# Weight blocks behind the rows' gather, one tile of softmax sums, a fourth staging tile

## The chip, the cores and the metric

The kernel runs on one core of one Trainium2 chip. The metric is the device time of one execution in microseconds (us): the median of several runs for the time, and one profiled execution for everything that is read from the trace. The engines are TensorE (PE; PEld its weight loads), VectorE (DVE), ScalarE (ACT), GpSimd (POOL) and SyncE (SP, which here issues most DMAs). Each takes its instructions in order.

## The reference

Three stages follow each other over 4 x 576 = 2304 tokens of width 512.

```python
# attention, 4 batches x 8 heads, 576 positions, head width 64, factor 4
q_d, k_d, v_d = (mean over groups of 4 positions of q, k, v)
out_d   = softmax(q_d k_d^T / 8) v_d                    # pooled part: 144 x 144
out_up  = repeat(out_d, 4, axis=positions)
scores  = where(abs(i - j) < 4, q k^T / 8, -1e9)        # banded part
x       = out_up + softmax(scores) v                    # heads side by side: 2304 x 512
# a dense product layer
x       = (((x @ w1) * (x @ w2)) @ w3) @ w_out          # inner width 1024
# a mixture of 8 experts, each token goes to one
e       = argmax(x @ w_gate)
g       = max(softmax(x @ w_gate)) * sigmoid((x @ w_output_gate)[e])
out     = g * relu(x @ e_w1[e]) @ e_w2[e]               # 512 -> 1024 -> 512
```

## The kernel before, in words

Every large product is made of three matmuls (`mm3`, lines 399 to 401): both factors are split into a high part (a cast on ScalarE) and a low part (a subtraction on VectorE or GpSimd), and high x high, high x low and low x high are added in PSUM.

**Weights at the front.** The four weights of the dense layer come in as 64-bit floats. `f64_bits` (lines 128 to 130) makes 32-bit floats of them with three VectorE instructions a tile. w_out is converted first, with w_gate and w_output_gate folded in (`gate_step`), then w3 is multiplied with it (`w3_part`, `wc_half`, `wc_out`) into `wc`, then w1 and w2 go through `w_part` in 16 pieces: `f64_bits` into a tile `wf`, a cast on ScalarE (line 377) and a subtraction on GpSimd (line 378). The tile `wf` of `w_part` and the tile `a` of `g1_step` (line 427: ScalarE's copy of the first product; line 428: VectorE multiplies with the second; 430: cast; 432: subtraction, on GpSimd for most) take turns in the staging tiles with the tag `t2k`, 2 KB a partition each, of which there are three. The tiles `wot`, `gs`, `ci` and `cj` have the same tag.

**Attention.** Two heads are one unit, 16 units in all. A unit goes through five steps, `a_T`, `a_S1`, `a_S2`, `a_V1`, `a_V2`, spread by hand between the steps of the dense layer (`step`). `a_S1` makes both score blocks: the banded one in `sm`, the pooled one in `ed`; ScalarE takes exponentials, and for `ed` it also writes the row sums to `zd` (line 217). `a_S2` reduces `sm` to its sums `su` (VectorE, 226), adds the epsilon and inverts (227, 228), and multiplies `sm` by the result on GpSimd (229); `zd` goes through the same two VectorE instructions (230, 231; there the factor 4 of the pooled mean is put in) and `ed` is multiplied on GpSimd (232). `a_V1` transposes `ed` on TensorE and `sm` on VectorE (244), `a_V2` multiplies with v; ScalarE copies the pooled output to `up` (272) and VectorE adds the two parts into `xr` (280).

**Dense layer.** Six groups of 384 tokens: `g1_step` (48 in all) and `g2_step`, which stores the rows of y to DRAM (`yd`; the second half of the width also to `yh`), and collects the gate logits. `route_*` make the tables of which token goes to which expert.

**The start of the experts.** The last part of the program is ordered by hand: `ordered(...)` puts a step's TensorE instructions behind those of the one before, `after(last)` puts ScalarE's and VectorE's behind a pair of theirs, `behind(rows, load)` makes a load wait until a gather has landed. Everything else is laid out by a planner that runs at build time with simulated times. The rows of the first expert are gathered from DRAM by GpSimd (`x_gather`, line 677) in two halves of the width, the second half first, and transposed into `xT` by `x_prep` (TensorE 695; ScalarE's cast and VectorE's subtraction 699). Expert weights come in blocks (r, m, i): expert rank r, first (m = 0) or second (m = 1) layer, block i of 4, 512 KB each; `ew_load` issues the load on SP (708 for m = 0, 711 for m = 1), `ew_split` casts on ScalarE (720) and subtracts on VectorE or GpSimd (722). The second-layer blocks of the first expert, (0,1,0) to (0,1,2), are loaded into the three parts of a tile `early`, the others into four tiles `raw`. While the first halves of the rows are on their way, `ga_part` runs the products of six column blocks with the second halves. `route_gate`, `gate_rhs` (573) and `route_gtab` (582, 585) make the table of gate values, and `route_gates` adds its parts (638, tile `b_gt`). Then the first halves are transposed (3 blocks of up to 128 rows, 2 PSUM tiles with the tag `tr`), `ga_step` finishes the first layer, `gb_step` does the second, and the loop over the other experts goes on; `x_gather(r + 1)` is issued on GpSimd behind the instruction called `first`.

Of the kernel before, what the change touches and what calls it, by code (L numbers as in the profile page):

```python
# [20 lines left out]
P = 128  # L21
# [3 lines left out]
G = 384  # L25
# [23 lines left out]
def attention_moe_kernel(ctx: ExitStack, tc: tile.TileContext, q, k, vw_in, v4_in, w1, w2, w3, w_out,  # L49
# [29 lines left out]
    ci = mt([P, P], I32, "ci", tag="t2k", bufs=3)  # L79
    cj = mt([P, P], F32, "cj", tag="t2k", bufs=3)  # L80
# [65 lines left out]
    for t in (kz, *qTs, bd, qz):  # L146
        nc.gpsimd.memset(t, 0.0)
    st = {}
# [40 lines left out]
    def a_S1(u):  # L189
# [24 lines left out]
        zd = at([96, 3], F32, "zd", bufs=2)  # L214
# [4 lines left out]
        d.update(sm=sm, ed=ed, zd=zd)  # L219

    def a_S2(u):
        d = st[u]
        sm, ed = d["sm"], d["ed"]
        su = at([P, 6, 2], F32, "su", bufs=2)
        sd = d["zd"]
        nc.vector.tensor_reduce(out=su, in_=sm, axis=AX.X, op=ALU.add)
        nc.vector.tensor_scalar(su, su, 1e-9, None, op0=ALU.add)
        nc.vector.reciprocal(su, su)
        nc.gpsimd.tensor_tensor(sm, sm, su.unsqueeze(3).to_broadcast([P, 6, 2, 32]), op=ALU.mult)
        nc.vector.tensor_scalar(sd, sd, 4.0, 4e-9, op0=ALU.mult, op1=ALU.add)  # L230
        nc.vector.reciprocal(sd, sd)
        nc.gpsimd.tensor_tensor(ed, ed, sd.unsqueeze(2).to_broadcast([96, 3, 144]), op=ALU.mult)
# [24 lines left out]
    def a_V2(u):  # L257
# [14 lines left out]
        nc.scalar.copy(out=up, in_=xl[0][:, 288:432])  # L272
# [43 lines left out]
    def gate_step(f, gps, src):  # L316
# [11 lines left out]
        wot = mt([P, KD, P], F32, "wot", tag="t2k", bufs=3)  # L328
# [5 lines left out]
    def gate_finish(gps):  # L334
        gs = mt([P, 2 * P], F32, "gs", tag="t2k", bufs=3)
# [32 lines left out]
    def w_part(m, f):  # L368
# [4 lines left out]
        t = mt([P, 512], F32, "wf", tag="t2k", bufs=3)  # L373
# [41 lines left out]
    def g1_step(g, f):  # L415
        xh, xl = xg[g]
        pp = []
        for m in range(2):
# [6 lines left out]
            if m == 0:  # L425
                a = mt([P, G], F32, "a", tag="t2k", bufs=3)
                nc.scalar.copy(out=a, in_=ps[:, 0:G])  # L427
# [253 lines left out]
    def x_prep(r, b, k0=0, k1=KD):  # L681
# [10 lines left out]
        ps = at_psum()  # L692
        pv = ps[:, 0:512].rearrange("p (k n) -> p k n", k=KD)
        for kk in range(k0, k1):
            nc.tensor.transpose(pv[:, kk, 0:n], t[0:n, P * kk:P * kk + P], ident[0:n, 0:n])  # L695
        c = slice(P * b, P * b + n)
        x = pv[:, k0:k1, 0:n]
# [291 lines left out]
    behind(rows, ew_load(0, 1, 0, early[:, 0]))  # L989
# [5 lines left out]
    store = ordered(g2_step, NG - 1, 2, 0)  # L995
    with tc.issue_after(store.ins):
        ew_load(0, 1, 1, early[:, 1])
    rows = x_gather(0, 0)
    behind(rows, ew_load(0, 0, 3))
    last = ordered(x_prep, 0, NBLK[0] - 1, KD // 2, KD)  # L1000
    with after(last):
# [5 lines left out]
        ew_split(0, 1, 0)  # L1007
# [4 lines left out]
    with tc.issue_after(rows.ins):  # L1012
        first = ew_split(0, 1, 1)
    for b in range(NBLK[0]):
        last = ordered(x_prep, 0, b, 0, KD // 2)
    with after(last):
        ew_split(0, 0, 3)
    for i in range(2, 4):
        behind(rows, ew_load(0, 1, i, early[:, 2] if i == 2 else None))
# [90 lines left out]
```

## Time and profile before

| | |
|---|---|
| median of 3 runs | 733.3 us (730.72 to 735.91) |
| profiled execution | 732.85 us |
| its span, first to last instruction | 731.0 us |
| busy: TensorE | 696.0 us, 95% |
| busy: VectorE | 434.1 us, 59% |
| busy: GpSimd | 324.7 us, 44% |
| busy: ScalarE | 282.5 us, 39% |
| mean granted TensorE clock | 0.99 |
| moved by DMA | 97.72 MB |

Times in the trace count from the first instruction. The profiled execution's own time is its span and 1.85 us around it. A busy TensorE is the time in which a matmul was under way, so what it lacks to the span are its waits. In a timeline, the bracket at the end of a line is how long the engine had been idle before the instruction, and what released it.

### The profile page before, as it was taken

The page shows a single profiled execution, that of the slowest core. Times are in us where ns is not written, and L with a number is a line of the kernel's source. Part 1 is how long each engine was busy: PE and PEld are TensorE (multiplying, and loading weights), DVE is VectorE, ACT ScalarE, POOL GpSimd, SP SyncE. Part 2 cuts the span into 40 slices and gives each one's busy share as a digit, 9 for nine tenths or more (in the row PEclk, how much of TensorE's full clock was granted, in tenths as well). Part 3 has the DMA queues.
Part 4 walks back from the last instruction along what each step waited for, and adds up shares of the span by engine and source line. Part 5 has one row for each costly group of instructions (what it writes and reads, how often), then busy time and mean ns, then how long its engine had stood idle before and what let it go on. Part 6 is the DMA issues. An engine that isn't in the chain of part 4 may idle for free.

```text
span 731.0 us, 14702 instructions
## 1 busy us (share of the span) xinstructions
PE 696.0 (95%) x5710; PEld 666.4 (91%) x5711; DVE 434.1 (59%) x924; ACT 282.5 (39%) x640; POOL 324.7 (44%) x306
## 2 busy tenths in 40 slices
PE   4889899999999999999999999979999999999995
PEld 3679788889999999999999999969999999999994
DVE  8999898862664547254352343475766656766830
ACT  3466356431354135135123121345353444544510
POOL 6866686930362155042011120166484655764611
PEclk9999999999999999999999999989999999999998
DMA  8987957512153032111100101665444744645301
GB/s 323 274 247 234 293 175 230 168 57 66 50 142 119 30 109 83 65 39 45 52 15 1 44 1 52 199 232 195 154 165 147 255 163 167 206 165 204 117 25 41
DMA packets 38264, 97.72 MB, mean 134 GB/s; under 512 B 6018, under 2 KB 12930, under 8 KB 38192
## 3 DMA queue, kind: packets, MB, share of 16 engines
q1 hardware_dynamic: 34768, 86.82, 36.5%
q0 software_dynamic: 3424, 9.93, 3.8%
q8 instruction: 46, 0.75, 0.4%
q14 instruction: 26, 0.21, 0.1%
HBM read 84.93 MB, written 12.29 MB: 133 GB/s over the span
## 4 chain that ended last, share of the span: by engine, by line
PE 73%; DMA 8%; POOL 5%; DVE 5%; issue 5%; ACT 2%; SPq 0%; POOLq 0%; DVEq 0%; ACTq 0%
PE g L399 22%; PE g L401 21%; PE g L400 21%; DMA v<-in_v_dram 3%; DMA kz<-in_k_dram 2%; PE at L197 1%; PE tr L695 1%; PE at L269 1%; PE at L209 1%; PE tr L788 1%; POOL v L236 1%; DMA f<-in_moe_w_dram 1%; POOL W L378 1%; PE at L265 1%; POOL out_dram L778 1%
## 5 line engine op out<-in xcount | busy, mean ns | idle before, releaser
L399 PE MATMUL g<-xh,W 128*128 128x384 f32 x384 | 131.7, 343 | 1.5 <-ACT a L427 1.4
L401 PE MATMUL g<-xh,W 128*128 128x384 f32 x384 | 129.4, 337 | 0.7 <-POOL W L378 0.7
L400 PE MATMUL g<-xl,W 128*128 128x384 f32 x384 | 129.3, 337 | 0.0
L722 DVE TENSOR_TENSOR W<-raw,W 128x1024 fp32r<-128x1024 f32 x32 | 87.9, 2779 | 34.0 <-ACT W L720 25.1
L722 POOL TENSOR_TENSOR W<-raw,W 128x1024 fp32r<-128x1024 f32 x29 | 82.9, 2877 | 36.2 <-ACT W L720 36.2
L432 POOL TENSOR_TENSOR h<-a,h 128x384 fp32r<-128x384 f32 x30 | 30.8, 1026 | 123.9 <-ACT h L430 123.7
L399 PE MATMUL g<-xT,W 128*128 128x288 f32 (+6 forms) x256 | 81.7, 319 | 1.0 <-ACT xT L699 1.0
L400 PE MATMUL g<-xT,W 128*128 128x288 f32 (+6 forms) x256 | 79.8, 312 | 0.0
L401 PE MATMUL g<-xT,W 128*128 128x288 f32 (+6 forms) x256 | 79.5, 311 | 0.0
L399 PEld LDWEIGHTS g<-xh,W 128*128 128x128 f32 x384 | 72.2, 188 | 4.2 <-ACT a L427 2.1
L401 PEld LDWEIGHTS g<-xh,W 128*128 128x128 f32 x384 | 72.1, 188 | 1.5 <-POOL W L378 1.3
L400 PEld LDWEIGHTS g<-xl,W 128*128 128x128 f32 x384 | 72.2, 188 | 0.0
L399 PE MATMUL g<-h,W 128*128 128x288 f32 (+5 forms) x224 | 69.9, 312 | 0.0
L400 PE MATMUL g<-wc,h 128*128 128x272 f32 (+1 forms) x240 | 68.4, 285 | 0.0
L399 PE MATMUL g<-wc,h 128*128 128x272 f32 (+1 forms) x240 | 68.3, 285 | 0.0
L400 PE MATMUL g<-h,W 128*128 128x288 f32 (+5 forms) x224 | 68.0, 303 | 0.0
L401 PE MATMUL g<-h,W 128*128 128x288 f32 (+5 forms) x224 | 68.0, 303 | 0.0
L401 PE MATMUL g<-wc,h 128*128 128x272 f32 (+1 forms) x240 | 67.7, 285 | 0.0
L428 DVE TENSOR_TENSOR a<-g,a 128x384 f32<-128x384 f32 x48 | 26.7, 555 | 62.8 <-PE g L401 58.6
L720 ACT CAST W<-raw 128x1024 fp32r<-128x1024 f32 x61 | 59.8, 1046 | 9.8 <-DMA raw<-in_moe_w_dram 5.6
L748 ACT ACTIVATE h<-g 128x288 fp32r<-128x288 f32 (+6 forms) x64 | 27.9, 436 | 77.2 <-PE g L401 71.7
L778 POOL DMA_INDIRECT out_dram<-orow,b_si x24 | 23.4, 976 | 62.9 <-DVE orow L777 59.4
(255 smaller groups left out, 1696.7 us busy)
## 6 DMA issues: line engine op xcount, KB each, us to landing
raw<-in_moe_w_dram SPq DMA_DIRECT2D x61, 512.0 KB, 4.2
f64w<-in_moe_w_dram SPq DMA_DIRECT2D x16, 512.0 KB, 4.5
f<-in_moe_w_dram SPq DMA_DIRECT2D x16, 512.0 KB, 3.5
vw<-in_vw_dram SPq DMA_DIRECT2D x16, 384.0 KB, 4.0
kc<-in_k_dram SPq DMA_DIRECT2D x16, 288.0 KB, 3.2
qT<-in_q_dram SPq DMA_DIRECT2D x16, 288.0 KB, 4.1
kz<-in_k_dram SPq DMA_DIRECT2D x32, 144.0 KB, 4.0
v<-in_v_dram SPq DMA_DIRECT2D x16, 288.0 KB
```

Of the source, the lines that this page charges most:

```text
L197: end = nc.tensor.matmul(sl[32 * j:32 * j + 32, b], qT[:, 24 * g:24 * g + 32], kz[:, :, 24 * g:24 * g + 32], start=True, stop=True, tile_p ...
L209: nc.tensor.matmul(sd[:, qb], qf[:, 96 * qb:96 * qb + 96], d["kd"], start=True, stop=True)
L236: nc.gpsimd.tensor_tensor(vt, vt, v4[:, :, 2:4], op=ALU.add)
L399: nc.tensor.matmul(ps, whi, xhi, start=first, stop=False)
L400: nc.tensor.matmul(ps, whi, xlo, start=False, stop=False)
L401: return nc.tensor.matmul(ps, wlo, xhi, start=False, stop=last)
L428: nc.vector.tensor_tensor(a, pp[1][:, 0:G], a, op=ALU.mult)
L432: eng.tensor_tensor(lo, a, hi.bitcast(F32), op=ALU.subtract)
L720: nc.scalar.copy(out=hi, in_=t)
L722: ins = eng.tensor_tensor(lo, t, hi.bitcast(F32), op=ALU.subtract)
L748: return nc.scalar.activation(out=t[:, 0, 0:C], in_=ps[:, 0:C], func=AF.Relu), nc.vector.scalar_tensor_tensor(t[:, 1, 0:C], ps[:, 0:C], 0. ...
L778: ins = nc.gpsimd.indirect_dma_start(out=out, out_offset=bass.IndirectOffsetOnAxis(ap=rt["si"][0:n, r, b:b + 1], axis=0), in_=t[0:n], in_o ...
```

## The change

Four edits, made together:

- The staging tag `t2k` has four tiles in place of three.
- The sums of both softmaxes of a unit lie in one tile of 15 columns, one tile for even and one for odd units: 12 for the banded part, 3 for the pooled one. One VectorE instruction adds the epsilon to all of them and one inverts all. The tiles are filled with ones at the start. `ed` is scaled by ScalarE, in three instructions with a scale per row, where GpSimd multiplied it. The factor of a quarter goes into ScalarE's copy `up`.
- The loads of (0,1,0) and (0,1,1), issued before the gather of the first halves, now come behind it, and their splits behind the transposes of the first halves.
- For the transposes of the first halves, two PSUM tiles are taken at once, and blocks 0 and 1 write different columns of the first.

The diff, without the hunks that only put `bufs=4` in place of `bufs=3` elsewhere:

```diff
@@ -145,6 +145,9 @@
     qz = at([P, 2, 144], F32, "qz")
     for t in (kz, *qTs, bd, qz):
         nc.gpsimd.memset(t, 0.0)
+    sums = [at([P, 15], F32, f"sum{i}") for i in range(2)]
+    for t in sums:
+        nc.vector.memset(t, 1.0)
     st = {}
 
     def burst():
@@ -211,25 +214,24 @@
         md = at([96, 3], F32, "md")
         nc.vector.tensor_reduce(out=md, in_=sd, axis=AX.X, op=ALU.max)
         nc.scalar.mul(md, md, -1.0 / 128)
-        zd = at([96, 3], F32, "zd", bufs=2)
+        zd = sums[u % 2][0:96, 12:15]
         nc.scalar.activation(out=sm, in_=sm, func=AF.Exp, scale=0.125)
         for qb in range(3):
             nc.scalar.activation(out=ed[:, qb], in_=sd[:, qb], func=AF.Exp, scale=1.0 / 128,
                                  bias=md[:, qb:qb + 1], accum_out=zd[:, qb:qb + 1])
-        d.update(sm=sm, ed=ed, zd=zd)
+        d.update(sm=sm, ed=ed)
 
     def a_S2(u):
         d = st[u]
         sm, ed = d["sm"], d["ed"]
-        su = at([P, 6, 2], F32, "su", bufs=2)
-        sd = d["zd"]
+        sums_u = sums[u % 2]
+        su = sums_u[:, 0:12].rearrange("p (b h) -> p b h", b=6)
         nc.vector.tensor_reduce(out=su, in_=sm, axis=AX.X, op=ALU.add)
-        nc.vector.tensor_scalar(su, su, 1e-9, None, op0=ALU.add)
-        nc.vector.reciprocal(su, su)
+        nc.vector.tensor_scalar(sums_u, sums_u, 1e-9, None, op0=ALU.add)
+        nc.vector.reciprocal(sums_u, sums_u)
         nc.gpsimd.tensor_tensor(sm, sm, su.unsqueeze(3).to_broadcast([P, 6, 2, 32]), op=ALU.mult)
-        nc.vector.tensor_scalar(sd, sd, 4.0, 4e-9, op0=ALU.mult, op1=ALU.add)
-        nc.vector.reciprocal(sd, sd)
-        nc.gpsimd.tensor_tensor(ed, ed, sd.unsqueeze(2).to_broadcast([96, 3, 144]), op=ALU.mult)
+        for qb in range(3):
+            nc.scalar.activation(out=ed[:, qb], in_=ed[:, qb], func=AF.Copy, scale=sums_u[0:96, 12 + qb:13 + qb])
         v4 = d["v4"]
         vd = at([72, 2, 2, D], F32, "vd", bufs=2)
         vt = v4[:, :, 0:2]
@@ -269,7 +271,7 @@
                     nc.tensor.matmul(xl[c // 3][64 * h:64 * h + 64, 96 * (c % 3):96 * (c % 3) + 96], vw[:, c, D * h:D * h + D],
                                      bd[:, 2 * c + h, :], start=True, stop=True)
         up = at([P, 144], F32, "up")
-        nc.scalar.copy(out=up, in_=xl[0][:, 288:432])
+        nc.scalar.mul(up, xl[0][:, 288:432], 0.25)
         for a in range(2):
             n = b * S + 288 * a
             assert G * split[0] >= n + 288 - RING
...
@@ -370,7 +372,7 @@
         if f % 2 == 0:
             for z in range(2):
                 wab[m][z][f // 2] = w_tile(8 * m + 4 * z + f // 2, [P, 1024])
-        t = mt([P, 512], F32, "wf", tag="t2k", bufs=3)
+        t = mt([P, 512], F32, "wf", tag="t2k", bufs=4)
         f64_bits(src, t.bitcast(U32))
         hi, lo = (wab[m][z][f // 2].rearrange("p (k c) -> p k c", k=KD)[:, :, P * (f % 2):P * (f % 2) + P] for z in range(2))
         x = t.rearrange("p (k c) -> p k c", k=KD)
@@ -678,7 +680,7 @@
                                                in_offset=bass.IndirectOffsetOnAxis(ap=idx, axis=0))
         return ins
 
-    def x_prep(r, b, k0=0, k1=KD):
+    def x_prep(r, b, k0=0, k1=KD, bank=None):
         C = CAPS[r]
         if r not in xT:
             if r == 0:
@@ -689,12 +691,12 @@
                 xT.update({i: (odd[:, 0], odd[:, 1]) for i in range(1, E, 2)})
         n = min(P, C - P * b)
         t = rt["xr"][r, b]
-        ps = at_psum()
-        pv = ps[:, 0:512].rearrange("p (k n) -> p k n", k=KD)
+        pv = (at_psum() if bank is None else bank)[:, 0:512].rearrange("p (k n) -> p k n", k=KD)
+        o = 0 if bank is None else (b % 2) * (k1 - k0)
         for kk in range(k0, k1):
-            nc.tensor.transpose(pv[:, kk, 0:n], t[0:n, P * kk:P * kk + P], ident[0:n, 0:n])
+            nc.tensor.transpose(pv[:, o + kk, 0:n], t[0:n, P * kk:P * kk + P], ident[0:n, 0:n])
         c = slice(P * b, P * b + n)
-        x = pv[:, k0:k1, 0:n]
+        x = pv[:, o + k0:o + k1, 0:n]
         hi, lo = xT[r][0][:, k0:k1, c], xT[r][1][:, k0:k1, c]
         return nc.scalar.copy(out=hi, in_=x), nc.vector.tensor_tensor(lo, x, hi.bitcast(F32), op=ALU.subtract)
 
@@ -986,17 +988,16 @@
     ordered(g2_step, NG - 1, 0, 0)
     rows = x_gather(0, 1)
     behind(rows, ew_load(0, 0, 2))
-    behind(rows, ew_load(0, 1, 0, early[:, 0]))
     ew_split(0, 0, 0)
     ordered(g2_step, NG - 1, 1, 0)
     for b in range(NBLK[0] - 1):
         ordered(x_prep, 0, b, KD // 2, KD)
     ew_split(0, 0, 1)
-    store = ordered(g2_step, NG - 1, 2, 0)
-    with tc.issue_after(store.ins):
-        ew_load(0, 1, 1, early[:, 1])
+    ordered(g2_step, NG - 1, 2, 0)
     rows = x_gather(0, 0)
     behind(rows, ew_load(0, 0, 3))
+    for i in range(2):
+        behind(rows, ew_load(0, 1, i, early[:, i]))
     last = ordered(x_prep, 0, NBLK[0] - 1, KD // 2, KD)
     with after(last):
         ew_split(0, 0, 2)
@@ -1004,19 +1005,20 @@
         rhs = mt([P, CPG, 2 * E * NC], F32R, "rhs", tag="W15")
         for c in range(CPG):
             gate_rhs(NG - 1, c, rhs[:, c])
-        ew_split(0, 1, 0)
     for f in range(6):
         ordered(ga_part, 0, f, KD // 2, KD, True, False)
     ordered(route_gtab, NG - 1, rhs)
     route_gates()
-    with tc.issue_after(rows.ins):
-        first = ew_split(0, 1, 1)
+    banks = [at_psum() for _ in range(2)]
     for b in range(NBLK[0]):
-        last = ordered(x_prep, 0, b, 0, KD // 2)
+        last = ordered(x_prep, 0, b, 0, KD // 2, banks[b // 2])
     with after(last):
         ew_split(0, 0, 3)
     for i in range(2, 4):
         behind(rows, ew_load(0, 1, i, early[:, 2] if i == 2 else None))
+    for i in range(2):
+        with after(last), tc.issue_after(rows.ins):
+            first = ew_split(0, 1, i)
     for r in range(E):
         for f in range(KF):
             last = ordered(ga_step, r, f)
```

## Rows read from the trace of the kernel before

**Rows 1.** Two windows: length, busy us (instructions) per engine, granted clock, DMA share, GB/s

```profile
20.00:160.00 140.00, 127.89 (x1371) 116.24 (x1372) 123.40 (x256) 73.10 (x199) 99.99 (x111) 0.99 0.70 216
160.00:470.00 310.00, 310.00 (x2598) 302.61 (x2597) 138.72 (x442) 93.28 (x249) 75.69 (x88) 1.00 0.20 60
```

**Rows 2.** Waits before 160 us: engine, line, releaser, us in total, times, longest

```profile
DVE wf L130 <- POOL h L432: 2.5, 2, 1.9
...
PE g L399 <- ACT a L427: 1.4, 2, 0.8
...
PE g L401 <- POOL W L378: 0.7, 2, 0.4
```

**Rows 3.** Timeline of VectorE, 99 to 100 us: start, length, instruction, idle before and releaser

```profile
99.11 0.15 DVE L230 TENSOR_SCALAR zd<-zd 96x3 f32<-96x3 f32 x1
99.19 0.15 DVE L227 TENSOR_SCALAR su<-su 128x12 f32<-128x12 f32 x1
```

**Rows 4.** Groups before 160 us: line, instruction, count, busy us, mean ns, idle before

```profile
L217 ACT ACTIVATE ed<-at,md 96x144 f32<-96x144 f32 x24 | 8.8, 370 | 0.1
...
L232 POOL TENSOR_TENSOR ed<-ed,zd 96x432 f32<-96x432 f32 x8 | 7.2, 905 | 3.7 <-ACT wc L363 2.0 <-DVE zd L231 1.6
```

**Rows 5.** Timeline of SP's DMA issues around the gathers, 450 to 515 us

```profile
468.39 1.01 SPq L711 DMA_DIRECT2D early<-in_moe_w_dram  x1
469.50 1.57 SPq L457 DMA_DIRECT2D yd<-yb  x2
```

**Rows 6.** Timeline of GpSimd, 476 to 482 us

```profile
476.13 1.23 POOL L677 DMA_INDIRECT xr<-yd,b_g  x1 [11.47 <-DMA early<-in_moe_w_dram]
477.66 0.95 POOL L677 DMA_INDIRECT xr<-yd,b_g  x1 [0.30 <-issue]
...
479.92 2.35 POOL L722 TENSOR_TENSOR W<-early,W 128x1024 fp32r<-128x1024 f32 x1
```

**Rows 7.** Timeline of VectorE, 475 to 483 us

```profile
475.29 1.23 DVE L722 TENSOR_TENSOR W<-early,W 128x1024 fp32r<-128x1024 f32 x1 [0.43 <-ACT W L720]
...
477.91 1.20 DVE L573 TENSOR_TENSOR rhs<-r_o,r_eb 128x288 fp32r<-128x288 f32 x3
...
480.10 2.34 DVE L638 TENSOR_TENSOR b_gt<-tab 128x144 f32<-128x144 f32 x1
```

**Rows 8.** Timeline of TensorE, 478 to 484 us

```profile
478.51 1.06 PE L582 MATMUL tr<-rhs,rb 128*128 128x288 f32 x3 [1.23 <-DVE rhs L573]
...
480.56 0.45 PE L695 MATMUL tr<-ident,xr 128*128 128x128 f32 x2 [0.77 <-DMA xr<-yd,b_g]
482.83 0.58 PE L695 MATMUL tr<-ident,xr 96*128 96x96 f32 x2 [1.82 <-DVE xT L699]
483.82 0.66 PE L399 MATMUL g<-xT,W 128*128 128x352 f32 x1 [0.41 <-ACT xT L699]
```

**Rows 9.** Timeline of ScalarE: the cast of the last late block of w1

```profile
485.34 1.04 ACT L720 CAST W<-raw 128x1024 fp32r<-128x1024 f32 x1 [1.57 <-DMA raw<-in_moe_w_dram]
```

**Rows 10.** Windows around the expert start, and one early stretch (columns of rows 1)

```profile
75.00:80.00 5.00, 2.17 (x53) 1.98 (x57) 4.75 (x10) 2.60 (x10) 2.55 (x5) 1.00 1.02 246
...
477.00:484.00 7.00, 2.77 (x12) 1.43 (x10) 6.28 (x16) 1.22 (x4) 5.90 (x6) 0.77 0.32 95
484.00:487.60 3.60, 3.60 (x12) 3.49 (x13) 1.34 (x3) 1.82 (x3) 2.51 (x3) 0.50 1.01 390
487.60:495.00 7.40, 7.40 (x48) 7.40 (x48) 4.67 (x9) 4.16 (x8) 2.41 (x1) 1.00 1.01 353
```

**Rows 11.** Timeline of all engines, 41 to 43 us: one PSUM bank written and read

```profile
41.67 0.67 PE L269 MATMUL at<-bd,vw 128*64 128x96 f32 x12
...
42.38 0.28 ACT L272 COPY up<-at 128x144 f32<-128x144 f32 x1 [1.25 <-PE at L269]
```

**Rows 12.** DMA issues, 450 to 467 and 480 to 500 us: count, size, landing

```profile
yh<-yb SPq DMA_DIRECT2D x2, 128.0 KB, 2.6
...
xr<-yd,b_gi POOLq DMA_INDIRECT x4, 7.8
```

More of the change, by code (lines that the diff above doesn't have):

```diff
@@ L78, in attention_moe_kernel @@
     i8 = i128[:, 0:E]
-    ci = mt([P, P], I32, "ci", tag="t2k", bufs=3)
-    cj = mt([P, P], F32, "cj", tag="t2k", bufs=3)
+    ci = mt([P, P], I32, "ci", tag="t2k", bufs=4)
+    cj = mt([P, P], F32, "cj", tag="t2k", bufs=4)
     nc.vector.memset(ones, 1.0)
@@ L327, in gate_step @@
             nc.tensor.transpose(ps[:, P * n:P * n + P], t[:, P * n:P * n + P], ident)
-        wot = mt([P, KD, P], F32, "wot", tag="t2k", bufs=3)
+        wot = mt([P, KD, P], F32, "wot", tag="t2k", bufs=4)
         nc.scalar.copy(out=wot, in_=ps.rearrange("p (n f) -> p n f", n=KD))
@@ L334, in gate_finish @@
     def gate_finish(gps):
-        gs = mt([P, 2 * P], F32, "gs", tag="t2k", bufs=3)
+        gs = mt([P, 2 * P], F32, "gs", tag="t2k", bufs=4)
         nc.scalar.copy(out=gs, in_=gps[:, 0:2 * P])
@@ L425, in g1_step @@
             if m == 0:
-                a = mt([P, G], F32, "a", tag="t2k", bufs=3)
+                a = mt([P, G], F32, "a", tag="t2k", bufs=4)
                 nc.scalar.copy(out=a, in_=ps[:, 0:G])
```

## The prediction

> **What bounds the kernel now.** I read the busy times by window first. From 160 to 470 us TensorE is busy in all of 310.00 us [rows 1]: nothing that another engine does there can shorten the run. From 20 to 160 us TensorE is busy 127.9 of 140, so 12.1 us are to be had, and VectorE, busy 123.4, is nearest to full; GpSimd has 100.0 and ScalarE 73.1 [rows 1]. Then the waits of that stretch: TensorE waited 1.4 us for ScalarE's copy `a` and 0.7 us for a GpSimd weight split, and VectorE 2.5 us, in two waits, for GpSimd's line 432, which frees a 2 KB staging tile [rows 2]. Last the timelines around the start of expert 0, since the other hole lies there: from 477 to 484 TensorE is busy 2.77 us of 7.0, and in the 3.6 us behind it the granted clock is 0.50, the 1.2 GHz level [rows 10].
>
> That second hole reads as a chain. SP issues the early block of w2 at 468.39, and the last two stores of y only from 469.50 on, ending at 471.07 [rows 5]. The gather of the rows' first halves, which needs those stores, starts at 476.13, after 11.47 us of idle GpSimd put down to the early blocks [rows 6]. Meanwhile VectorE splits the early block at 475.29, ahead of the gate chain, whose `rhs` ends at 479.11 [rows 7]; TensorE waits 1.23 us for it, then 0.77 for rows of block 1, then 1.82 for VectorE, and resumes expert 0 at 483.82 [rows 8]. VectorE was late because `b_gt` at 480.10 took 2.34 us [rows 7], under GpSimd's split of the second early block, 479.92 for 2.35 [rows 6]; the larger `rhs` products took 1.20/3 = 0.4 us each [rows 7].
>
> **The fourth staging tile (A).** It removes no instruction. VectorE's 2.5 us of waits were for a staging tile, and TensorE's 1.4 + 0.7 = 2.1 us came at the end of the weight conversion, which VectorE paces [rows 2]. Bounds: 0, if the planner, which orders all engines by simulated times at build, spends the tile otherwise, or if the next weights, loaded only as older ones are converted, are late instead; and -2.1. I take **-1.5**, nearer to the whole, since the wait removed from VectorE is longer than TensorE's.
>
> **The softmax (B).** Eight of the sixteen units fall before 160 us [rows 4]; the other eight lie under the full TensorE and are worth nothing. Each loses two small VectorE instructions (`zd` at lines 230 and 231). One occupies 0.08 us from start to start and 0.15 by its length [rows 3]: 8 x 2 x 0.08 = 1.3 us, at most 8 x 2 x 0.15 = 2.4. GpSimd loses 8 x 0.905 = 7.2 us; ScalarE gains 24 scalings, for which the nearest row is the exponential of the same shape, 0.370 us [rows 4], so up to 8.9 us on an engine with 67 to spare. In a unit's own chain three times 0.37 = 1.1 stand in place of 0.905, 0.2 worse, or 8 x 0.2 = 1.6 us if every unit were on the path. VectorE's add of epsilon now also waits for the three exponentials; behind it queue its weight conversions. Before, `zd` was ready 0.08 us ahead of that add [rows 3], so I cost the wait at nothing; without that cover it is up to three exponentials, 1.1 us, a unit. From +1.6 to -2.4 I take **-1.0**, VectorE's time, because VectorE is the fullest engine. The factor 0.25 rides on a copy that is there anyway. **C**: two fills of 15 columns on VectorE at the start, 0.1 at most, since even the 3-column `zd` lasts 0.15 [rows 3]: **+0.1** for both.
>
> **The rows earlier (D).** The early loads of (0,1,0) and (0,1,1) go behind the gather. So the last store, issued by 471.07, meets an emptier queue; a store of this size landed in 2.6 us [rows 12], at 473.7. The gather then starts 2.4 us earlier than 476.13. In it, block 1 started 1.53 us after block 0, and its rows were used at 480.56, 2.9 us after its start; all three were issued by 479.9 [rows 6, 8]. New: block 0 lands at 476.6, block 1 at 478.1, block 2 at about 479.4. The gate chain loses the 1.23 us split in front of it, the length of TensorE's wait, so its 1.06 us product runs from 477.3 to 478.35. Block 0's transposes follow. Blocks 0 and 1 now share a PSUM bank. The row of before in which a bank's other columns are still being written has ScalarE start at 42.38, behind matmuls that end at 42.34, though they write other columns than it reads [rows 11]; so block 1 waits for both readers of block 0, about 1.5 us from its start (TensorE resumed 0.99 us after block 2's transposes began, with one reader between [rows 8]; the second reader half as much again): 479.85, then 0.45, then block 2 at 480.3, and 0.99 later, 481.3, TensorE resumes. Gain 483.8 - 481.3 = **-2.5**. If the store lands no earlier, the shorter chain alone leaves block 2 at 476.13 + 5.7 = 481.8 and TensorE at 482.8: -1.0. If block 1 need not wait, block 2's landing at 479.4 sets it, TensorE resumes at 480.4: -3.4.
>
> The Trainium skill (PSUM — Partial Sum Buffer, "PSUM bank collisions raise a hardware error") speaks against this part: it has accesses of two engines guarded by bank and quadrant, not by address. By it the saving of a buffer is no saving of a wait, D = -2.5; by addresses alone it would be -3.4. The trace agrees with the guard, as the 42.38 row shows.
>
> **The clock (E).** Twelve matmuls took 3.60 us at 0.50 against 7.40/48 = 0.154 each at 1.00: 12 x (0.300 - 0.154) = 1.75 us lost [rows 10]. TensorE had been busy 2.77 of 7 us before that; earlier, 2.17 of 5 us left the clock at 1.00 [rows 10]. After the change it would be busy 1.06 + 0.45 + 0.45 + 0.4 of the 4.0 us to 481.3, which lies between: half, **-0.9**, with 0 and -1.75 as ends.
>
> **The weights later (F).** On SP the loads now wait for the gather's landing, 479.4, all four of w2 behind (0,0,3); expert 1's loads queue behind them. 0.524 MB at 390 GB/s [rows 10] is 1.34 us a block; with the store's 2.6 taken as the latency in front, (0,0,3) lands at 483.3, (0,1,1) at 486.0, (0,1,3) at 488.7. TensorE needs 60 matmuls x 0.155 before the second layer, 490.6, and 18 more, 493.4, before the last block. That block: cast 1.04 [rows 9], GpSimd split 2.35, done at 492.1 in 1.3 us of cover. In GpSimd's queue the gather of expert 1 stands behind the split of (0,1,1), done at 489.4; 1.5 us each [rows 6], one gather ahead of the last split costs 0.2, two 1.7. Rows for expert 1 are needed at 490.6 + 24 x 0.155 = 494.3: with the 2.9 us landing nothing, with 7.8, the median of 480 to 500 us [rows 12], 497.2 and 2.9 us of wait. ScalarE's relus may stand behind a cast; four PSUM buffers cover that. I take **+0.7**, nearer to none, because by 489 most of the loads have passed.
>
> Sum: -1.5 - 1.0 + 0.1 - 2.5 - 0.9 + 0.7 = -5.1. The profiled execution took 732.85 (span 731.0, 1.85 around it), 0.45 below the median 733.3: 732.85 - 5.1 = **727.75**.
>
> **Rivals.** (1) *The front gives nothing*: the planner lays out the order anew, the longer ScalarE chain eats VectorE's relief, A and B cancel. For it: eight units at +0.2; against: VectorE's buffer waits are plain in the rows. Without -2.5: 730.2. (2) *Slower: expert 1's rows come late.* GpSimd takes the split of (0,1,3) first, the gather starts at 492.1 and lands after 7.8 us, 499.9: TensorE waits 5.6 us behind the first part of expert 0's second layer, and the clock falls again, so E is 0. -1.5 - 1.0 + 0.1 - 2.5 + 5.6 + 1.75 = +2.45: 735.3. It decides from a landing at about 499.4, where wait and clock outweigh the -4.9. For it: 1 MB of loads moved into a stretch with the DMA at 390 GB/s; against: the queue is nearly drained by then. (3) *More than forecast*: both waits of TensorE at the front go (-2.1), B in full (-2.4), no half clock (-1.75), D as forecast, F 0: -8.65, 724.2. (4) *It does not do what it says*: the store lands no earlier behind the load (0,0,2), D = -1.0, E = 0: 730.15.
>
> **How the numbers follow.** Forecast 0.52, between 725 and 730; rivals (1) and (4) together 0.23, near 730; (3) 0.16; (2) 0.09. One per cent, about what a measurement of this kernel tells from no change, is 7.3 us: 726.0 and 740.6. Faster by over 1%: all of (3) and a third of the forecast that lies low, 0.16 + 0.15 = 0.31; slower by over 1%: only (2) with more on top, 0.04; the rest 0.65. The range reaches from beyond (3), where D's -3.4 adds to it, 723.3, to between (1) and (2), 733.5; what lies outside are most of (2) and the ends of (3).
>
> **What would show it.** Right: no VectorE wait at line 130 for line 432; L232 gone from GpSimd and three short ScalarE instructions a unit in its place; first-half gather starting within 3 us of the last store; `b_gt` near 0.3 us; TensorE resuming some 4 us after its first-half products, with less or no half clock. Wrong: a wait of TensorE at line 695 for rows of expert 1, or at line 399 or 401 for a split, between 490 and 500 us; or as much idle before 160 us as now.

## The result and the profile after

| | before | after |
|---|---|---|
| median of 20 runs | 733.75 us (730.21 to 737.59) | 737.16 us (733.87 to 743.62) |
| ratio of the times, 95% interval | | 1.0069 [1.0048, 1.0089] |
| profiled execution | 732.85 us | 739.67 us, span 737.8 |
| busy: TensorE, VectorE | 696.0, 434.1 us | 699.0, 425.1 us |
| busy: GpSimd, ScalarE | 324.7, 282.5 us | 308.7, 296.4 us |

By the ratio, the change made the kernel slower by 0.69%, some 5 us (the two medians differ by 3.4 us), where 5.6 us less than the median was forecast. The measured time lies above the range.

The windows of after that answer to [rows 1], and three from the start of the experts on:

```profile
20.00:160.00 140.00, 125.33 (x1344) 114.50 (x1345) 119.09 (x236) 78.30 (x217) 91.40 (x103) 0.96 0.69 215
160.00:470.00 310.00, 310.00 (x2588) 302.31 (x2587) 136.63 (x426) 100.30 (x273) 68.73 (x81) 1.00 0.19 59
...
485.00:495.00 10.00, 9.27 (x57) 8.98 (x57) 6.01 (x7) 7.26 (x12) 3.62 (x2) 1.00 1.00 390
500.00:505.00 5.00, 2.40 (x9) 2.33 (x10) 0.00 (x0) 0.45 (x1) 4.99 (x4) 0.64 0.44 116
505.00:510.00 5.00, 5.00 (x23) 5.00 (x23) 1.92 (x2) 1.63 (x2) 3.14 (x2) 0.68 0.94 343
```

The front shows the main loss. VectorE has 4.3 us less to do than in [rows 1] (119.09 for 123.40) and GpSimd 8.6 us less (91.40 for 99.99), as the diff promises. Yet TensorE gets 27 fewer matmuls done (1344 for 1371), in 2.6 us less busy time at a mean clock of 0.96 instead of 0.99. The relieved engines stand idle, and TensorE waits more. The clock has a share beside the waits. From 20 to 60 and from 60 to 100 us, before:

```profile
20.00:60.00 40.00, 34.71 (x458) 30.24 (x460) 37.68 (x89) 23.28 (x70) 31.52 (x40) 0.96 0.84 256
60.00:100.00 40.00, 36.91 (x470) 34.46 (x467) 35.62 (x77) 21.05 (x64) 24.56 (x30) 1.00 0.84 259
```

After:

```profile
20.00:60.00 40.00, 35.08 (x455) 31.16 (x456) 33.38 (x79) 23.16 (x71) 28.16 (x36) 0.91 0.84 246
60.00:100.00 40.00, 35.60 (x439) 33.04 (x438) 32.29 (x66) 24.10 (x67) 20.15 (x25) 0.96 0.75 240
```

That is some 7 us more at the 1.2 GHz level (the mean clock is lower by 0.05 and 0.04 over 40 us each, and that level is half of the other), so by estimate up to 3.5 us lost, of one size with the 2.6 us of waits. Since TensorE is full from 160 us to the experts, whatever is left undone at 160 comes back behind it, one for one. The cleanest clock for this is the first gather of the new rows on GpSimd, which starts when the last products of the dense layer are nearly through. Before:

```profile
461.01 1.16 POOL L677 DMA_INDIRECT xr<-yh,b_gi  x1 [23.88 <-PE g L400]
```

After (lines are shifted by 2 to 3 in this kernel):

```profile
465.30 1.17 POOL L679 DMA_INDIRECT xr<-yh,b_gi  x1 [23.88 <-PE g L402]
...
478.58 0.96 POOL L679 DMA_INDIRECT xr<-yd,b_g  x1 [9.62 <-DVE r_gs L561]
...
491.23 2.39 POOL L724 TENSOR_TENSOR W<-early,W 128x1024 fp32r<-128x1024 f32 x1 [9.06 <-ACT W L722]
493.77 1.78 POOL L679 DMA_INDIRECT xr<-yd,b_gi  x1
...
498.30 1.87 POOL L679 DMA_INDIRECT xr<-yd,b_gi  x1 [0.30 <-issue]
500.18 7.00 POOL L724 TENSOR_TENSOR W<-raw,W 128x1024 fp32r<-128x1024 f32 x3
```

That gather is 4.29 us late, so by then 4.3 of the 6.8 us between the two profiled spans are lost. The waits of the front that are new or longer (engine, line, releaser, us in total, times, longest):

```profile
ACT ed L234 <- DVE sum L231: 9.2, 4, 6.1
...
DVE sT L246 <- POOL sm L232: 4.2, 4, 1.5
...
PE at L267 <- ACT pt L256: 2.3, 1, 2.3
...
PE at L200 <- DVE wc L366: 2.1, 1, 2.1
```

VectorE's wait for line 432 fell from 2.5 us [rows 2] to 0.3, nearly as forecast. In its place ScalarE stands 9.2 us in front of the new scalings, and TensorE now waits for attention copies and for `wc`. The longest of ScalarE's waits can be followed on VectorE:

```profile
105.49 0.55 DVE L229 TENSOR_REDUCE sum<-sm 128x12 f32<-128x384 f32 x1
...
106.88 5.04 DVE L395 TENSOR_TENSOR xl<-xr,xh 128x384 fp32r<-128x384 f32 x2
111.84 0.16 DVE L230 TENSOR_SCALAR sum<-sum 128x15 f32<-128x15 f32 x1
...
113.37 0.23 DVE L231 RECIPROCAL sum<-sum 128x15 f32<-128x15 f32 x1
```

The sum is there at 106.04, its add comes at 111.84 and the reciprocal at 113.37: the planner laid other work between them. Most of it is the row of 5.04 us, two subtractions of 384 columns for the first group's rows (before: 1.88 us); the last section comes back to it. ScalarE's in-order queue stands meanwhile:

```profile
107.19 0.37 ACT L365 CAST wc<-g 128x256 fp32r<-128x256 f32 x1
113.70 1.03 ACT L234 ACTIVATE ed<-ed,sum 96x144 f32<-96x144 f32 x3 [6.13 <-DVE sum L231]
```

### The profile page after: what moved, and what is told of

Its sections match the earlier page's. It is cut to its first block, busy times and chain, and to the rows that moved or that the text cites. A ratio compares the mean times of both kernels' runs of the same rounds, so it can differ in the third digit from the quotient of the medians.

```text
span 737.8 us, 14695 instructions
## 1 busy us (share of the span) xinstructions
PE 699.0 (95%) x5710; PEld 669.7 (91%) x5711; DVE 425.1 (58%) x894; ACT 296.4 (40%) x688; POOL 308.7 (42%) x290
## 4 chain that ended last, share of the span: by engine, by line
PE 72%; DMA 8%; POOL 7%; issue 6%; DVE 5%; ACT 1%; SPq 0%; POOLq 0%; DVEq 0%; ACTq 0%
PE g L401 21%; PE g L403 21%; PE g L402 21%; DMA v<-in_v_dram 3%; PE at L271 2%; DMA kc<-in_k_dram 1%; PE tr L697 1%; PE at L200 1%; PE at L212 1%; DMA kz<-in_k_dram 1%; PE tr L790 1%; POOL W L380 1%; PE at L267 1%; POOL W L724 1%; POOL xr L679 1%
## 5 line engine op out<-in xcount | busy, mean ns | idle before, releaser
L724 DVE TENSOR_TENSOR W<-raw,W 128x1024 fp32r<-128x1024 f32 x32 | 84.4, 2668 | 36.7 <-ACT W L722 34.8
L403 PE MATMUL g<-h,W 128*128 128x288 f32 (+5 forms) x224 | 69.2, 309 | 3.5 <-POOL W L724 3.5
L401 PE MATMUL g<-h,W 128*128 128x288 f32 (+5 forms) x224 | 71.0, 317 | 0.0
L402 PE MATMUL g<-h,W 128*128 128x288 f32 (+5 forms) x224 | 68.9, 308 | 0.0
L401 PEld LDWEIGHTS g<-xT,W 128*128 128x128 f32 x256 | 48.2, 188 | 2.4 <-ACT xT L701 1.3
```

Of the source, the lines that this page charges most:

```text
L401: nc.tensor.matmul(ps, whi, xhi, start=first, stop=False)
L402: nc.tensor.matmul(ps, whi, xlo, start=False, stop=False)
L403: return nc.tensor.matmul(ps, wlo, xhi, start=False, stop=last)
L724: ins = eng.tensor_tensor(lo, t, hi.bitcast(F32), op=ALU.subtract)
```

## The experiments

All ran five rounds against the kernel before. Three theories stood at first: the softmax edit's own waits cost (1), the new start of the experts costs (2), any new layout of the front by the planner costs (3).

**The parts.** `e1_start_only` is the kernel before with the hunks of the expert start alone:

```diff
-    behind(rows, ew_load(0, 1, 0, early[:, 0]))
...
+    for i in range(2):
+        behind(rows, ew_load(0, 1, i, early[:, i]))
...
+    banks = [at_psum() for _ in range(2)]
...
+    for i in range(2):
+        with after(last), tc.issue_after(rows.ins):
+            first = ew_split(0, 1, i)
```

> The attention and the staging tiles as before; only the start of expert 0 is changed (loads of (0,1,0) and (0,1,1) behind the gather, shared PSUM bank). Theory 1, the split of block (0,1,3) stands behind four gathers in GpSimd's queue and eats what the earlier rows give: TensorE resumes expert 0 about 3.5 us sooner, then waits about 3.5 us at the second layer and runs some 4 us at the half clock: 1 to 2.5 us slower than before. Rival, all of the loss is made in the front and the start is a gain: 2 to 4 us faster than before.

Measured: 731.92 us beside 733.03, ratio 0.9994 [0.997, 1.0019]. The start costs nothing and brings nothing that can be told from noise; both theories had expected a difference.

`e2_front_only` has all the rest of the change and the old start:

```diff
+    sums = [at([P, 15], F32, f"sum{i}") for i in range(2)]
...
+            nc.scalar.activation(out=ed[:, qb], in_=ed[:, qb], func=AF.Copy, scale=sums_u[0:96, 12 + qb:13 + qb])
...
-        t = mt([P, 512], F32, "wf", tag="t2k", bufs=3)
+        t = mt([P, 512], F32, "wf", tag="t2k", bufs=4)
```

> The start of the experts as before; shared sums, ScalarE's scaling and four staging tiles as changed. Theory 1, ScalarE stands still for VectorE's reciprocal with its other work behind it: 1 to 4 us slower than before, idle ScalarE at the scaling line of some 9 us before 160 us. Rival, the front is not slower and the profiled execution was a bad one: within 1 us or up to 2 us faster.

Measured: 735.85, ratio 1.0057 [1.0032, 1.0081]. The loss is in the front.

`e3_staging_only` has the fourth tile alone, `e4_softmax_only` the softmax alone:

```diff
# e3, and so for the other tiles of the tag
-    ci = mt([P, P], I32, "ci", tag="t2k", bufs=3)
+    ci = mt([P, P], I32, "ci", tag="t2k", bufs=4)
# e4
-        zd = at([96, 3], F32, "zd", bufs=2)
+        zd = sums[u % 2][0:96, 12:15]
```

> Only the fourth staging tile. Theory 1, it takes VectorE's and TensorE's waits away: 0.5 to 2 us faster. Rival, any new plan of the front costs some us whatever the edit: 1 to 4 us slower.

> Only the shared sums and ScalarE's scaling; three staging tiles and the start as before. Theory 1, this edit is what costs the front: 1 to 4 us slower than before. Rival, it is the staging tile or the plan: within 1 us of before.

Measured: 732.22, 0.999 [0.997, 1.0011] for the tile, and 736.81, 1.0055 [1.0032, 1.0079] for the softmax. The softmax edit alone carries the loss. In the tile's build the order of instructions on every engine but ScalarE is that of before, and one there has another place.

**Which half of the softmax.** `e5_shared_gpsimd` keeps the shared sums and leaves the scaling of `ed` to GpSimd; `e6_separate_scalare` keeps the separate sums and scales on ScalarE:

```diff
# e5, on top of the softmax edit
-        for qb in range(3):
-            nc.scalar.activation(out=ed[:, qb], in_=ed[:, qb], func=AF.Copy, scale=sums_u[0:96, 12 + qb:13 + qb])
+        nc.gpsimd.tensor_tensor(ed, ed, sums_u[0:96, 12:15].unsqueeze(2).to_broadcast([96, 3, 144]), op=ALU.mult)
# e6, on the kernel before
-        nc.gpsimd.tensor_tensor(ed, ed, sd.unsqueeze(2).to_broadcast([96, 3, 144]), op=ALU.mult)
+        for qb in range(3):
+            nc.scalar.activation(out=ed[:, qb], in_=ed[:, qb], func=AF.Copy, scale=sd[:, qb:qb + 1])
```

> Only the shared tile of sums (three staging tiles, the start as before); the pooled scores are still multiplied on GpSimd. Theory 1, the cost is the coupling: one addition and one inversion wait for the slower of the two softmaxes, so 2 to 4 us slower than before, as with the whole edit. Theory 2, the cost is the scaling on ScalarE, whose queue stands still for it: within 1 us of before. Theory 3, it is the new plan as such: anything between, unrelated to the other runs.

> Separate sums as before, only the scaling of the pooled scores moves from GpSimd to ScalarE. Theory 1, coupling: within 1 us of before. Theory 2, ScalarE: 2 to 4 us slower, with some 8 us of idle ScalarE ahead of the scaling before 160 us. Theory 3, the new plan: as in e5.

Measured: 738.21, 1.0088 [1.006, 1.0115], and 735.75, 1.0053 [1.003, 1.0076]. Either half alone costs as much as both. Two independent costs would add, so neither ScalarE's scaling nor the joint sum is *the* cause.

**A change of nearly nothing.** `e7_replanned` is the kernel before with one small VectorE instruction more a unit, `e12_two_step_scale` with one small ScalarE instruction more:

```diff
# e7
-        nc.vector.tensor_scalar(sd, sd, 4.0, 4e-9, op0=ALU.mult, op1=ALU.add)
+        nc.vector.tensor_scalar(sd, sd, 4.0, None, op0=ALU.mult)
+        nc.vector.tensor_scalar(sd, sd, 4e-9, None, op0=ALU.add)
# e12
-        nc.scalar.mul(md, md, -1.0 / 128)
+        nc.scalar.mul(md, md, -1.0)
+        nc.scalar.mul(md, md, 1.0 / 128)
```

> The kernel before with one more VectorE instruction a unit: the factor 4 and the epsilon of the pooled sums in two instructions in place of one, 0.08 us each. The plan of the front comes out anew. Theories 1 and 2: 0 to 0.7 us slower, eight units before 160 us at 0.08. Theory 3, a new plan costs by itself: 2 to 4 us slower, or faster.

> The kernel before, with the scaling of the row maxima of the pooled scores in two ScalarE instructions in place of one, some 0.2 us more of ScalarE a unit, 3.5 us in all on an engine that is busy for 39%. If any new plan of the front costs: 736 to 738 us. If it was VectorE's extra instruction that cost in the replanned run before: within 1.5 us of the kernel before.

Measured: 735.99, 1.0063 [1.0041, 1.0084], and 736.69, 1.0061 [1.004, 1.0082]. For eight units in the front, 0.08 us each of VectorE [rows 3] is 0.6 us; the price is over 4 us. It is not the instruction's time.

**Same edit, another place or table.** `e9_moved_unit` and `e10_moved_unit_softmax` move one entry of the table of attention steps, without and with the softmax edit; `e16_softmax_table_b` and `e15_softmax_table_c` are the softmax edit with two other tables:

```diff
# e9, e10
# (the first row of G1STEP)
-[1, 1, 2, 1, 2, 1, 2, 2]
+[1, 2, 1, 1, 2, 1, 2, 2]
# e16
+[1, 1, 1, 1, 2, 2, 2, 2]
# e15 (the last four of W3STEP)
-(1, 1, 1), (1, 1, 1), (1, 1, 0), (1, 1, 0)
+(1, 1, 0), (1, 1, 1), (1, 1, 1), (1, 1, 0)
```

> The kernel before, with one entry of the hand-set table of attention steps moved: the second step that stood behind the third column block of the first group's g1_step stands behind the second. No instruction is added or taken away; the planner lays the front anew. If any new plan of the front costs 4 to 6 us (the theory that the runs so far point to): 736 to 738 us beside some 732.5 of the kernel before. If only the softmax edit's own waits cost: within 1 us of the kernel before.

> The same moved entry, and the softmax edit on top (shared sums, ScalarE's scaling, the quarter in up). To be read against the run with the moved entry alone. If the edit only loses the plan that the tables were set for, its price is gone here: within 1.5 us of the moved entry alone. If its own waits (ScalarE's scaling behind VectorE's sums, some 19 us in sum on ScalarE before 160 us) set the end, it is 4 us slower than the moved entry alone again.

> The softmax edit with the attention steps of the first group's g1_step spread 1, 1, 1, 1, 2, 2, 2, 2 in place of 1, 1, 2, 1, 2, 1, 2, 2. As in the run before: within 1.5 us of the kernel before if the edit lost only the tables' fit and this one happens to fit, 3 to 5 us slower if its own chain costs.

> The softmax edit with one attention step moved from behind the fifth column block of the w3 phase to behind the seventh. If the edit only lost the tables' fit, some tables fit it again: within 1.5 us of the kernel before. If its own chain costs: 3 to 5 us slower than before, whatever the table.

Measured: e9 733.08, 1.0018 [0.9997, 1.0038]; e10 736.56, 1.0061 [1.0041, 1.0082]; e16 737.03, 1.0069 [1.0046, 1.0093]; e15 738.46, 1.0087 [1.0062, 1.0111]. My expectation for e9 rested on an error: compared instruction by instruction, the built program stands in the same order as before on every engine, and e10 and e16 stand in that of e4. So e9 says nothing on a new layout; e10 and e16 are repeats of e4 and show how firm its 0.55% is. Only e15 has another order, and is no faster (the intervals overlap).

**Extra work in or out of the chain, and less work.** `e13_side_step` adds ScalarE's small instruction beside the chain of the softmax; `e14_no_maximum` leaves the row maxima of the pooled scores out of the computation:

```diff
# e13
         nc.scalar.mul(md, md, -1.0 / 128)
+        nc.scalar.mul(side_t, side_t, 1.0)
# e14
-        nc.vector.tensor_reduce(out=md, in_=sd, axis=AX.X, op=ALU.max)
-        nc.scalar.mul(md, md, -1.0 / 128)
...
-                                 bias=md[:, qb:qb + 1], accum_out=zd[:, qb:qb + 1])
+                                 accum_out=zd[:, qb:qb + 1])
```

> The kernel before with one more ScalarE instruction a unit (0.2 us on a 96x3 tile of its own that nobody reads), beside the scaling of the row maxima and not in the chain of the softmax. Same work of ScalarE as the two-step scaling, which cost 4.2 us. If a longer chain inside a unit is what costs: within 1.5 us of the kernel before. If the extra instruction only makes the planner lay the front anew, in or out of the chain: 3 to 5 us slower, as with the two-step scaling.

> The kernel before without the row maxima of the pooled scores (VectorE's reduction, ScalarE's scaling and the bias of the exponentials are left out): a shorter chain in each unit, some 0.6 us of VectorE and 0.2 us of ScalarE less a unit, 9 and 3 us in all. If the length of the chain sets the front: 3 to 8 us faster. If the front is as good as it is because the tables were set for just this work, any other plan being worse: slower by up to 4 us in spite of less work.

Measured: 732.63, 1.0001 [0.9982, 1.0021] for the side step; 737.27, 1.007 [1.0048, 1.0091] for less work. The side step was fitted in without moving any other instruction. It depends on nothing, and the planner put all sixteen between 5.8 and 13.6 us, where ScalarE had idle time; so this run shows that an edit which leaves the order alone is free, and not what the same work would cost inside a unit. Without the maxima, two instructions and a dependence a unit are gone and the kernel is 5 us slower: a longer chain cannot be what costs here. Its front (the columns of [rows 1]; gather on GpSimd below):

```profile
20.00:160.00 140.00, 126.88 (x1351) 115.51 (x1351) 120.72 (x245) 68.48 (x187) 101.15 (x112) 0.96 0.70 216
```

```profile
464.79 1.16 POOL L674 DMA_INDIRECT xr<-yh,b_gi  x1 [23.89 <-PE g L397]
```

Twenty matmuls fewer by 160 us than in [rows 1], and the gather 3.8 us late, with less work on VectorE and ScalarE.

**Order and work exchanged.** In the last two, the order of one kernel is written out on every engine and the other kernel's instructions are put into it:

```diff
+    for e, (size, stretches) in PLAN.items():
+        mine = [...]  # this engine's instructions, as the program names them
+        turn = [k for a, n in stretches for k in range(a, a + n)]
+        for x, y in zip(turn, turn[1:]):
+            tc.add_manual_dep(mine[y], mine[x].name, dep, reason="the order, written out")
```

> The softmax edit alone, with the kernel before's order of instructions written out by hand on every engine (each instruction behind its predecessor of that order); only VectorE's three instructions on the sums and ScalarE's three scalings of a unit, which the kernel before has not in this form, are left to the planner. If the edit costs 4 us because it makes the planner lay the front anew: within 1.5 us of the kernel before, 0.5 to 1 us faster if the instructions that it saves are worth what the prediction gave them. If the edit's own waits cost: 3 to 5 us slower, as without the written order.

> The counterpart: the kernel before, none of its instructions changed, in the order that the planner gave the softmax edit, written out on every engine; VectorE's sums and GpSimd's multiplication of the pooled part are left to the planner where the edit has no counterpart. If the order is what costs: 3 to 5 us slower than the kernel before. If the edit's own instructions and waits cost: within 1.5 us.

Measured: 735.69, 1.0083 [1.005, 1.0117] for the edit in the old order; 739.89, 1.0117 [1.0094, 1.014] for the old work in the edit's order. So theory (3) in its plain form falls too: if the order alone were at fault, the old order would have cured the edit. And the old work pays 8.6 us in the edit's order, so a loss does not need the edit's own instructions. That each order holds only for the work that it was laid for fits both, but it is not shown: what only one of the two kernels has (VectorE's instructions on the sums, ScalarE's or GpSimd's scaling) was left to the planner in both runs. The edit in the old order meets a wait of its own on GpSimd, before 160 us:

```profile
POOL sm L234 <- DVE sum L233: 6.0, 3, 2.6
```

Before, GpSimd's waits for VectorE were 0.8 us in all at that line. The prediction's wait, VectorE's for the pooled exponentials, is something else: before 160 us it is 0.19 us, once, in this run, and nothing in after. Ahead of GpSimd's longest wait here (2.55 us, until 101.82) ScalarE is through with the exponentials at 99.15, and other work of VectorE stands between its three instructions on the sums:

```profile
98.95 0.20 ACT L222 ACTIVATION_READ_ACCUMULATOR ed<-at,md 96x1 f32 x1
...
99.37 0.55 DVE L231 TENSOR_REDUCE sum<-sm 128x12 f32<-128x384 f32 x1
...
100.69 0.17 DVE L232 TENSOR_SCALAR sum<-sum 128x15 f32<-128x15 f32 x1
...
101.41 0.24 DVE L233 RECIPROCAL sum<-sum 128x15 f32<-128x15 f32 x1
```

TensorE is as busy from 20 to 160 us in this run as before (128.08 us for 127.89), so what this wait costs is not shown. The counterpart has waits of another kind (ScalarE):

```profile
ACT sm L217 <- POOL sm L205: 13.3, 4, 8.6
```

Line 217 there is line 215 of before, whose longest such wait was 3.8 us.

**The start mended.** In after, the split of (0,1,3) stands on GpSimd behind four gathers (the 500.18 row above). `e8_gather_behind_split` is e1 with the gathers for expert 1 behind that split, `e11_start_and_staging` adds the fourth staging tile:

```diff
-                        ew_split(r, 1, 2 + f // 2)
+                        first = ew_split(r, 1, 2 + f // 2)
```

> The start of e1 (front as before), with the gather of expert 1 on GpSimd behind the split of (0,1,3). Theory 1, that split behind four gathers is what eats the gain of the earlier rows: no wait of TensorE for it, 2.5 to 5 us faster than before. Rival, expert 1's rows come late in its place: TensorE waits at their transposes by 2 us or more, within 1.5 us of before.

> The start of the experts as changed, with the gather of the second expert's rows behind the split of (0,1,3), and the fourth staging tile; the softmax as before. If the two add up: 0.3 to 0.4% faster, 730.0 to 730.5 us beside 732.5. If the staging tile's tenth of a per cent was nothing: 0.28%, 730.6. If the gain of the start hangs on one chip's runs: ratio 0.999 to 1.0.

Measured: 730.96 beside 731.8, 0.9972 [0.9945, 1.0]; and 730.27 beside 732.5, 0.997 [0.995, 0.999]. e8's 2.0 us are less than the 2.5 to 5 that were expected, and its interval ends at no change; e11, with the same start, is clear of it, so it is faster than both kernels. The tile's tenth is not to be told from nothing in it. GpSimd in e8:

```profile
484.63 2.39 POOL L722 TENSOR_TENSOR W<-early,W 128x1024 fp32r<-128x1024 f32 x1 [9.10 <-ACT W L720]
487.23 3.15 POOL L722 TENSOR_TENSOR W<-raw,W 128x1024 fp32r<-128x1024 f32 x1 [0.20 <-ACT W L720]
490.52 0.97 POOL L677 DMA_INDIRECT xr<-yd,b_gi  x1
```

And TensorE there, its only waits between 478 and 514 us:

```profile
484.91 0.43 PE L399 MATMUL g<-xT,W 128*128 128x352 f32 x1 [0.64 <-DVE h L748]
489.46 0.43 PE L399 MATMUL g<-h,W 128*128 128x352 f32 x1 [0.45 <-DVE h L748]
494.71 0.63 PE L695 MATMUL tr<-ident,xr 128*128 128x128 f32 x4 [1.15 <-DMA xr<-yd,b_gi]
```

The wait for the split is gone, no half clock follows (1.00 in all windows from 477 to 505), and the later gathers cost 1.15 us.

**All profiles together.** The start of the first gather of new rows, one profile each:

```
order of before on TensorE:  before 461.01, e1 463.13, e3 458.77, e8 458.79, e9 460.00, e11 459.03, e13 462.93
another order:               after 465.30, e2 462.64, e4 464.15, e10 465.32, e16 465.30 (these five nearly alike),
                             e5 464.74, e6 466.76, e7 463.26, e12 464.02, e14 464.79, e15 464.04, e18 468.09
edit in the order of before: e17 464.80
```

Seven profiles in the old order with the old softmax have a mean of 460.5; the twelve in another order have 464.9: some 4.4 us, the size of the measured losses. The two groups overlap from 462.6 to 463.1, so one profile alone could not have told them apart.

## Why the prediction was wrong

**A, the staging tile: right in kind, its size not settled.** -1.5 was taken for the tile; it measured -0.1% [-0.3, +0.1], so -0.7 us, with -2.2 and +0.7 as ends. The interval holds both the -1.5 and "0, if the planner ... spends the tile otherwise". VectorE's wait at line 130 for line 432 did shrink in after.

**B, the softmax: the step that failed.** "From +1.6 to -2.4 I take -1.0, VectorE's time, because VectorE is the fullest engine." It measured +0.55% [0.32, 0.79], some +4.0 us, outside both ends. The savings themselves came: VectorE had 4.3 us less before 160 us, more than the 2.4 of the far end, and the GpSimd group was gone. The scalings that replace it (L234 beside L220, which answers to line 217 of [rows 4]):

```profile
L220 ACT ACTIVATE ed<-at,md 96x144 f32<-96x144 f32 x24 | 8.7, 369 | 0.2
...
L234 ACT ACTIVATE ed<-ed,sum 96x144 f32<-96x144 f32 x24 | 8.2, 404 | 9.2 <-DVE sum L231 9.2
```

Their busy time was sized well (8.9 forecast); their 9.2 us of waiting was not in the sum. What failed is adding instruction times to a schedule that was taken as fixed, and taking VectorE's saved time for TensorE's: instead of gaining 1.0, TensorE had 2.6 us less busy time in the front. "VectorE's add of epsilon now also waits for the three exponentials ... so I cost the wait at nothing" was read from one unit of the old order [rows 3], which was gone after the edit, yet it held: no such wait stands in after. The waits that came are those of ScalarE and GpSimd for VectorE's sums (9.2 and 2.2 us in after), between whose three instructions the new order laid other work. Rival (1) named the planner's new order, but priced it at no more than the cancelled gain; nothing was set aside for a worse order, so its price was missing from the range. The ablations, e7, e12 and e14 above all, show that the price is not that of any instruction; e17 and e18 that neither the order nor the work is enough as an explanation.

**C, the fills and the quarter:** no run has them alone.

**D, the rows earlier: right.** Against the first gather, 4.29 us later than before, TensorE resumes expert 0 at 484.60 where it was 483.82 [rows 8]: 3.5 us gained, for -2.5 forecast with -3.4 as the end. The gather of first halves starts 3.2 us behind the end of the last store's issue (475.35; within 3 was named; before, 5.1), and VectorE's `b_gt` took 0.31 us for 2.34 [rows 7], with no GpSimd split beside it. TensorE around the shared bank in after:

```profile
483.16 0.44 PE L697 MATMUL tr<-ident,xr 128*128 128x128 f32 x2 [1.01 <-DVE xT L701]
483.81 0.39 PE L697 MATMUL tr<-ident,xr 96*128 96x96 f32 x2 [0.21 <-DMA xr<-yd,b_g]
484.60 0.43 PE L401 MATMUL g<-xT,W 128*128 128x352 f32 x1 [0.41 <-ACT xT L701]
...
502.60 0.66 PE L403 MATMUL g<-h,W 128*128 128x352 f32 x1 [3.53 <-POOL W L724]
```

Block 1 waits 1.01 us for VectorE, which reads block 0's columns, before it writes its own in the same bank. The guard by bank that the Trainium skill tells of (PSUM — Partial Sum Buffer, "PSUM bank collisions raise a hardware error") agrees with that row.

**E, the clock: the end, not the middle.** The clock is 1.00 from 485 to 495, so -1.75 and not half of it. The half rested on "which lies between", and 2.36 of 4.0 us is a larger busy share than in either of the two rows it was set against (2.77 of 7, 2.17 of 5).

**F, the weights later: mechanism right, mis-sized.** "One gather ahead of the last split costs 0.2, two 1.7", and +0.7 was taken. All four gathers stood ahead of it, 493.77 to 500.17, and TensorE waited 3.53 us at 502.60. In that wait the clock fell: 0.64 and 0.68 in the windows to 510, so the 1.2 GHz level up to about 508.2 (0.68 of 5 us leaves 3.2 at half, with the 2.4 of busy TensorE before it 5.6 us, half of them lost): 2.8 us more. -3.5 - 1.75 + 6.3 = +1.1 from one profile (of the 2.5 us that are lost behind the gather, 1.4 stay unexplained); e1 measured -0.4 us [-2.2, +1.4] for D, E and F together, for -2.7 forecast. Rival (2) had this shape, a wait at the second layer and a second fall of the clock, but with rows of expert 1 as the late thing; the late thing was the split behind the gathers of those rows. e8 shows it: with the split first, the wait goes and 0.28% are gained, 0.30% [0.1, 0.5] in e11.

**Left open.** Which parts of the front's order make the 4 us no run settles. Three are seen, and none is in all slow orders. VectorE's slow subtractions (last section) are in the edit's own order and in e6. GpSimd's wait for the sums is 6.0 us in the old order and 6.9 in e4, but 2.2 in after, 2.6 in e7 and 1.2 in e15. The lower clock is in the edit's order: over all its runs e4 has a mean granted clock of 0.986 beside 0.990, some 6 us more at the 1.2 GHz level, so at most 3 of its 4 us by estimate. But e7 and e15 have neither the slow subtractions nor a long wait for the sums, e6, e7 and e12 keep the clock of before (0.990, 0.990 and 0.991), and all lose as much. Whether the edit could be laid out to cost nothing is open too: of the three layouts of it that were tried (its own, table C, the old order) none was free.

## What to carry to other kernels

In a stretch that a planner lays out, price an edit in two parts: its instructions, and the change of order that comes with it; here every edit that moved the order lost 4 to 6 us, one whose instructions are worth 0.6 us and one that leaves work out among them, and those that left TensorE's order alone lost nothing, but for the edit in the old order. Before believing a gain from a relieved engine, ask for an edit of nearly nothing that forces a new layout, and compare with that. And where work moves behind a gather on an in-order queue, count every gather that is issued there ahead of it: the start with one split put ahead of four of them was the only thing in this study that gained.

## What the runs showed of the hardware

VectorE's subtraction of 128x384 columns takes 0.55 us as the median, and several times that where GpSimd's elementwise instructions follow each other beside it. VectorE in after (duration: shortest, median, longest, ns):

```profile
L395 DVE TENSOR_TENSOR xl<-xr,xh x22: 495/553/3497, 106.9 to 406.3; 128x384 fp32r<-128x384 f32 x22
```

GpSimd beside the two long ones:

```profile
107.92 1.98 POOL L395 TENSOR_TENSOR xl<-xr,xh 128x384 fp32r<-128x384 f32 x2
109.86 1.64 POOL L380 TENSOR_TENSOR W<-wf,W 128x512 fp32r<-128x512 f32 x1
```

The pair took 1.86 to 1.88 us in all eight profiles in the order of before, e17 among them, and 4.1 to 5.5 us in all six in the edit's own order, e18 among them: it goes with the order, not with the work. It is worth up to 3.6 us on the fullest engine, but in e15 (1.01) and e7 (1.68) it is short, and they are slow too. In e15 GpSimd's two subtractions start behind VectorE's; in before they lie beside them and the pair is short all the same, so being side by side does not set the size. `b_gt`, 2.34 us under a GpSimd split [rows 6, 7] and 0.31 without, looks like the same thing at the other end.

The granted clock of the front differs from run to run in one and the same order. From 20 to 60 us, in e1:

```profile
20.00:60.00 40.00, 34.90 (x451) 30.76 (x452) 35.22 (x88) 22.62 (x69) 31.11 (x40) 0.91 0.85 255
```

and in e9:

```profile
20.00:60.00 40.00, 34.80 (x478) 29.90 (x480) 38.24 (x91) 24.28 (x72) 32.12 (x42) 1.00 0.86 266
```

27 matmuls more at 1.00 than at 0.91, in the same busy time. That is part of what lies between the first gathers of these two (463.13 and 460.00), and a reason to read a difference of 2 us in this kernel from rounds of runs and not from two profiles.
